# Softmax denominators from sums of four key tiles, and a planner with other durations

## The chip, the cores and the metric

The kernel runs on one core of a Trainium2 chip. Its time is the device time of one execution in microseconds (us). A core has five instruction queues that run beside each other: TensorE (PE; its weight loads are shown apart as PEld), VectorE (DVE), ScalarE (ACT), GpSimd (POOL) and SyncE (SP), which here issues the DMAs.

## The reference

One pre-norm transformer layer, S = 2048 tokens, D = 1024, 32 heads of 32, F = 3584, everything bf16 at its edges:

```
h  = x + softmax(q k^T / sqrt(32)) v @ wo      with q, k, v = layernorm(x) @ wqkv
h2 = h + (gelu_tanh(layernorm(h) @ w1 + b1) @ w2 + b2)
```

There is no mask; the layer norms have no scale and no offset.

## The kernel before

**Attention.** A job is one group `g` of four heads (4 x 32 = 128 rows) and one block `qb` of 256 queries; there are 8 x 8 = 64 jobs. A job has eight rounds `r`, each of two key tiles of 128 keys. A round first makes scores in `Att.qk` (line 769): eight matmuls, four at a time on 32-row strips of the array, into two of three score units of two PSUM banks (banks 0 to 5). Then two exponentials on ScalarE (line 779), one for each unit, 128 x 1024 each, write the probabilities to one of nine `PT` buffers. `Job.pv` (line 805) multiplies them with V, four matmuls at a time on 32-column strips, and accumulates into the left half of a bank (6 or 7); `Job.den` (line 834) multiplies them, or sums of them, with a matrix of ones, and accumulates the softmax denominators into the right half of the same bank. `Job.finish` (lines 850 to 865) transposes and inverts the denominators and scales the output on VectorE.

**The denominators.** For rounds 0 to 6 VectorE first adds the two key tiles of the round (the pair sum, line 820, 128 x 1024 bf16), into one of three `PS` buffers used in turn, and `den` then needs four matmuls for the round. Round 7 goes to `den` directly, with eight. The two jobs of the lead (`g` = 0, `qb` < 2) take all eight rounds directly. A sum that round r appends is handed to `den` in the call of `pv` for round r + 1, behind its value matmuls.

**The rest of the layer** is background work (kind "bg") that TensorE does between the rounds: the projections of Q, K and V, the output projection `wo(u)` of a block u of 256 tokens, `ln2(u)`, `ffn1(u)` and `ffn2(u)`. Their results leave PSUM through banks 6 and 7 only, mostly by VectorE (for `ffn1` line 943). The GELU of four 128-wide chunks is four VectorE instructions and one ScalarE tanh (lines 962 to 967, the tanh on 965), in two `uu` buffers. The last block's `wo(7)`, `ln2(7)`, `ffn1(7)`, `ffn2(7)` come after the last job and use all banks (line 540). In the lead (`lead_norm` and the loop over `hc`) the layer norms of x, the transposes, the first projections and the two lead jobs run interleaved.

**The planner.** Nothing of this order is written out. The kernel first builds a graph of tasks; each has an engine, a duration (`occ`), a latency until its result can be used (`lat`) and a priority. `Graph.schedule` then simulates the engines by these figures: when an engine comes free it takes the ready task of lowest priority number (pair sums have -2, PSUM evictions 0, GELU steps 1); TensorE's task is chosen by `pick_pe`: scores first, then a value round when three rounds wait, else background work. A change between strip shapes on TensorE costs `switch`. The order so found is emitted: five fixed queues, with semaphore waits between them. On the chip each engine works strictly down its queue, so a task whose input is late holds all that is queued behind it. The planner's figures come from the helper functions

```python
MM = 0.2195
def c_dve_ps(n): return (120 + n) / 960.0 + 0.02
def c_dve(n, x=1): return (62 + n / x) / 960.0 + 0.085
def c_act(n, ap_bias=False): return 0.073 + (0.093 if ap_bias else 0.0) + n / 1200.0
```

and from constants at the calls.

Of the kernel before, what the change touches and what calls it, by code (L numbers as in the profile page):

```python
# [60 lines left out]
class Graph:  # L61
# [46 lines left out]

    def schedule(self, pick_pe, pool, switch=0.1, dma_rate=280.0, dma_lat=2.1, dma_issue=0.06):
        for i, t in enumerate(self.tasks):  # L110
# [10 lines left out]
        n = 0  # L121
# [207 lines left out]
def build_kernel(nc, A_x, A_wqkv, A_wo, B_w1, B_b1, B_w2, B_b2, out):  # L329
# [156 lines left out]

    MM = 0.2195
    def c_dve_ps(n):
        return (120 + n) / 960.0 + 0.02

    def c_dve(n, x=1):
        return (62 + n / x) / 960.0 + 0.085

    def c_act(n, ap_bias=False):
        return 0.073 + (0.093 if ap_bias else 0.0) + n / 1200.0

    def pe(fns, occ, reads=(), writes=(), kind="bg", mode="full", prio=0, after=()):
        return gr.add(E.PE, fns, occ, 0.16, reads, writes, prio, kind, mode, after)

# [15 lines left out]
    def bb(bank):  # L515
        return bank.buf if isinstance(bank, Slot) else B_ps[bank]
# [10 lines left out]
    def mm(bank, lhsT, rhs, start, stop, reads, narrow, cols=(0, 512), after=()):  # L527

        c0, c1 = cols
        occ = MM * (c1 - c0) / 512.0 + 0.003  # L530
        if narrow:
            fns = []
            for j in range(4):
                fns.append(lambda p, j=j: p.matmul(psum[32 * j:32 * j + 32, bi(bank), c0:c1], lhsT[:, 32 * j:32 * j + 32], rhs,  # L534
                                                   start=start, stop=stop, tile_position=(0, 32 * j), skip_group_check=True))
            t = pe(fns, occ, reads=reads, writes=[bb(bank)], mode="col", after=after)
            t.whole = lambda p: p.matmul(psum[:, bi(bank), c0:c1], lhsT, rhs, start=start, stop=stop,  # L537
                                         skip_group_check=True)
        else:
            t = pe(lambda p: p.matmul(psum[:, bi(bank), c0:c1], lhsT, rhs, start=start, stop=stop),  # L540
                   occ, reads=reads, writes=[bb(bank)], mode="full", after=after)
        take(t, bank)

    def act(fn, n, reads=(), writes=(), prio=0, ap_bias=False, kind="", after=()):
        return gr.add(E.Activation, fn, c_act(n, ap_bias), 0.14, reads, writes, prio, kind, after=after)

    def dve(fn, occ, reads=(), writes=(), prio=0):
        return gr.add(E.DVE, fn, occ, 0.08, reads, writes, prio)

# [24 lines left out]
    def layer_norm(tiles, prio, norm="dve", stats=None):  # L574
# [6 lines left out]
        for k, (x_ap, B_x, o_ap, B_o) in enumerate(tiles):  # L581
            for c in range(2):
                dve(lambda v, c=c, k=k, x_ap=x_ap: v.bn_stats(st_l[:, i + k, 6 * c:6 * c + 6], x_ap[:, 512 * c:512 * c + 512]),
                    0.68, reads=B_x if isinstance(B_x, list) else [B_x], writes=[B_stl[i + k]], prio=(prio or 1) if stats is None else stats)
            dve(lambda v, k=k: v.bn_aggr(mv_l[:, i + k, :], st_l[:, i + k, :]), 0.2,  # L585
                reads=[B_stl[i + k]], writes=[B_mv[i + k]], prio=prio)
# [9 lines left out]
        for k, (x_ap, B_x, o_ap, B_o) in enumerate(tiles):  # L596
            eng, cost = (dve, 0.58) if norm == "dve" else (pool, 3.8)
            eng(lambda e, k=k, x_ap=x_ap, o_ap=o_ap: e.tensor_scalar(
                o_ap, x_ap, mvr[:, i + k, :], rden[:, i + k, :], ALU.subtract, ALU.mult), cost,
                reads=(B_x if isinstance(B_x, list) else [B_x]) + [B_mvr[i + k], B_rden[i + k]], writes=[B_o], prio=prio)  # L600

    def transposes(src_ap, B_src, bank, dst_ap, B_dst, evac, prio):
        for dc in range(DC):
            t = pe(lambda p, dc=dc: p.transpose(psb[:, bi(bank), dc * P:(dc + 1) * P], src_ap[:, dc * P:(dc + 1) * P], ident[:]),  # L604
                   0.064, reads=[B_src, B_ident], writes=[bb(bank)], prio=prio)
            take(t, bank)

        def src():
            return psb[:, bi(bank), :].rearrange("p (dc t) -> p dc t", dc=DC)
        if evac == "act":  # L610
            t = act(lambda a: a.activation(dst_ap, src(), ACT.Copy), 1024, reads=[bb(bank)], writes=[B_dst], prio=-1)  # L611
        else:
            t = dve(lambda v: v.tensor_copy(dst_ap, src()), 0.70, reads=[bb(bank)], writes=[B_dst])
        drop(t, bank)
# [132 lines left out]
    class Att:  # L747
# [8 lines left out]
        def qk(self, job, r):  # L756
# [16 lines left out]
            for u in us:  # L773
                banks += [B_ps[2 * u], B_ps[2 * u + 1]]
            pe(fns, 0.224, reads=[B_KT[8 * g + r], B_QT[qs]], writes=banks, kind="qk", mode="row")
            s = self.rounds % NR
# [9 lines left out]

    closing = set()

    class Job:
# [8 lines left out]
        def pv(self, r, s):  # L798
# [10 lines left out]
            rd = [B_PT[2 * s], B_PT[2 * s + 1], B_V[NT * g + 2 * r], B_V[NT * g + 2 * r + 1]]  # L809
            t = pe(fns, 0.224, reads=rd, writes=[self.B_O, self.B_D] if first else [self.B_O], kind="pv", mode="col")  # L810
            take(t, bank)
            while self.sums:
                self.den(*self.sums.pop(0), False)
            if r == 7 or (self.g == 0 and self.qb < 2):
                self.sums.append((s, True))
            else:
                n = cnt["ps"] % NS
                cnt["ps"] += 1
                pairs = PT[:, s, :, :, :].rearrange("p u j c -> p (u j) c")
                dve(lambda v: v.tensor_tensor(PS[:, n, :, :], pairs[:, :, 0:256], pairs[:, :, 256:512], ALU.add), c_dve(1024, 2),  # L820
                    reads=[B_PT[2 * s], B_PT[2 * s + 1]], writes=[B_PS[n]], prio=-2)
                self.sums.append((n, False))
            if last:
# [4 lines left out]
        def den(self, n, direct, last):  # L828
            bank = self.bank
            fns = []  # L830
            for i in range(2 if direct else 1):
                for h in range(4):
# [3 lines left out]
                        start=False, stop=last, tile_position=(0, 32 * h), skip_group_check=True))  # L836
            t = pe(fns, 0.224 if direct else 0.112, reads=[B_PT[2 * n], B_PT[2 * n + 1]] if direct else [B_PS[n]],
                   writes=[self.B_D], kind="den", mode="col")
# [3 lines left out]
        def finish(self):  # L842
# [6 lines left out]
            D = OD[:, o, 1, :].rearrange("p (b j) -> p b j", j=32)  # L849
            t = dve(lambda v: v.transpose(OD[:, o, 1, :], psum[:, bi(bank), 256:512]), 0.445,  # L850
                    reads=[self.B_O, self.B_D], writes=B_D, prio=-1)
# [7 lines left out]
            drop(t, bank)  # L859
            dve(lambda v: v.reciprocal(rr[:, o, :], D[:, :, 0]), 0.185, reads=B_D, writes=[B_rr[o]], prio=0)  # L860
            dve(lambda v: v.transpose(D, rr[:, o, :].unsqueeze(2).to_broadcast([P, 8, 32])), c_dve(256),
# [144 lines left out]
    for k in range(80):  # L1006
        pe(lambda p: p.matmul(psum[:, 6, 0:256], ident[:, :], b2t[:, 0:256], start=True, stop=True), 0.12,  # L1007
           reads=[B_ident, B_b2t], writes=[B_ps[6]], kind="warm")
# [243 lines left out]
```

## Time and profile before

| what | value |
|---|---|
| median of 3 runs | 1100.69 us (1100.36, 1100.69, 1102.47) |
| profiled execution, span of its instructions | 1099.2 us; its own time is given by this span alone, 1.5 us under the median of the runs |
| instructions | 42056 |
| TensorE busy | 1056.5 us, 96% |
| ScalarE busy | 1019.8 us, 93% |
| VectorE busy | 757.2 us, 69% |
| GpSimd busy | 47.8 us, 4% |
| first exponential starts, last exponential starts | 16.4 us, 1030.0 us |
| ScalarE idle before the exponentials, in all | 18.2 us |

A busy TensorE in this table is not TensorE at its peak: the matmuls overlap and their ends are modelled. "Idle before" is time in which the engine stood still ahead of an instruction, with what ended it. The exponentials of one queue overlap by their start-up, so their durations (some 1.2 us) add up to more than the time that they take: one follows the other every 0.92 us.

### The profile page before, as it was taken

The numbers are of one execution on the slowest core, as the hardware profiler recorded it, in microseconds if no ns is written. First come the engines' busy times: TensorE is split into PE (matmuls) and PEld (weight loads), VectorE is DVE, ScalarE is ACT, GpSimd is POOL, SyncE is SP. The second block draws the span as 40 slices with busy tenths as digits, with TensorE's granted clock in tenths as the row PEclk, the third lists the DMA queues.
The fourth block names the chain that finished last, engine by engine and source line by source line (L and its number), as shares of the span: only waits on it lengthen the run. The fifth ranks groups of instructions, "written<-read, shape, count | busy, mean of one in ns | idle before, by whom it ended". The sixth has DMA issues, their size and how long they took to land.

```text
span 1099.2 us, 42056 instructions
## 1 busy us (share of the span) xinstructions
PE 1056.5 (96%) x19177; PEld 613.8 (56%) x19226; DVE 757.2 (69%) x1444; ACT 1019.8 (93%) x1124; POOL 47.8 (4%) x110
## 2 busy tenths in 40 slices
PE   8899999998899999999999899999999999999998
PEld 6655555553345744664475456546744664565483
DVE  7746666665676886788588768876886787687501
ACT  3879999999999999999999999999999999999650
POOL 3200000000000001001000100010010000000100
PEclk9999999999899999999999999999999999999999
DMA  6820000048345654854576466448654747797370
GB/s 184 227 103 2 29 2 3 2 159 268 115 122 154 189 151 150 260 162 149 185 228 188 150 203 180 143 150 255 181 178 149 216 142 239 243 266 242 98 262 20
DMA packets 265506, 174.43 MB, mean 159 GB/s; under 512 B 26864, under 2 KB 260336, under 8 KB 264560
## 3 DMA queue, kind: packets, MB, share of 16 engines
q1 hardware_dynamic: 265328, 171.74, 51.2%
q8 instruction: 151, 2.47, 0.9%
q14 instruction: 27, 0.22, 0.1%
HBM read 161.23 MB, written 10.49 MB: 156 GB/s over the span
## 4 chain that ended last, share of the span: by engine, by line
ACT 79%; PE 19%; DVE 1%; issue 0%; DMA 0%; POOL 0%; POOLq 0%; DVEq 0%
ACT PT L779 75%; PE ps L540 6%; ACT uu L965 4%; PE ps L537 4%; PE ps L534 3%; PE ps L769 2%; PE ps L805 1%; PE ps L1007 1%; PE ps L834 1%; DMA a_w1r<-in_A_wo_dram 0%; ACT xnT L611 0%; PE ps L604 0%; DVE PS L820 0%; DVE OD L850 0%; DVE OD L857 0%
## 5 line engine op out<-in xcount | busy, mean ns | idle before, releaser
L779 ACT ACTIVATE PT<-ps 128x1024 bf16<-128x1024 f32 x1024 | 953.6, 1189 | 18.2 <-PE ps L769 18.0
L820 DVE TENSOR_TENSOR PS<-PT 128x1024 bf16<-128x1024 bf16 x434 | 287.5, 686 | 124.5 <-ACT PT L779 63.8
L769 PE MATMUL ps<-QT,KT 32*128 32x256 bf16 x4096 | 204.6, 273 | 13.5 <-ACT PT L779 10.2
L805 PE MATMUL ps<-PT,V 128*32 128x256 bf16 x4096 | 179.9, 273 | 1.5 <-ACT PT L779 1.1
L769 PEld LDWEIGHTS ps<-QT,KT 32*128 32x128 bf16 x4096 | 61.0, 92 | 174.1 <-ACT PT L779 165.3
L834 PE MATMUL ps<-PS,ones 128*32 128x256 bf16 x1736 | 121.7, 274 | 2.0 <-DVE PS L820 2.0
L805 PEld LDWEIGHTS ps<-PT,V 128*32 128x32 bf16 x4096 | 103.8, 97 | 30.0 <-issue 8.7
L537 PE MATMUL ps<-a_w2r,gT 128*128 128x512 bf16 x445 | 109.6, 380 | 4.9 <-issue 2.4
L537 PE MATMUL ps<-hnT,a_w1r 128*128 128x256 bf16 x903 | 111.2, 273 | 1.1 <-DVE rr L860 0.5
L534 PE MATMUL ps<-hnT,a_w1r 128*32 128x256 bf16 x2660 | 96.9, 274 | 2.4 <-DVE gT L943 1.2
L537 PEld LDWEIGHTS ps<-hnT,a_w1r 128*128 128x128 bf16 x903 | 82.7, 98 | 25.1 <-issue 14.8
L943 DVE TENSOR_TENSOR gT<-ps,b1f 128x512 bf16<-128x512 f32 x98 | 67.3, 687 | 27.7 <-PE ps L534 18.4
L534 PE MATMUL ps<-a_w2r,gT 128*32 128x512 bf16 x1140 | 81.6, 381 | 2.5 <-DVE OD L857 2.5
L534 PEld LDWEIGHTS ps<-hnT,a_w1r 128*32 128x32 bf16 x2660 | 66.2, 96 | 18.5 <-issue 14.0
L537 PEld LDWEIGHTS ps<-a_w2r,gT 128*128 128x128 bf16 x471 | 40.4, 98 | 55.3 <-issue 15.7
L989 DVE SCALAR_TENSOR_TENSOR hch<-ps,hch 128x512 bf16<-128x512 f32 x32 | 22.0, 689 | 64.0 <-PE ps L540 47.1
L834 PEld LDWEIGHTS ps<-PS,ones 128*32 128x32 bf16 x1736 | 45.9, 96 | 22.8 <-issue 8.7
L965 ACT ACTIVATE uu<-uu 128x1024 bf16<-128x1024 bf16 x49 | 58.0, 1206 | 0.0
L537 PE MATMUL ps<-xnT,Wall 128*128 128x512 bf16 (+1 forms) x213 | 47.7, 360 | 2.3 <-issue 1.1
L588 POOL CAST mvb<-mv 128x2 bf16<-128x2 f32 (+1 forms) x25 | 6.1, 242 | 990.0 <-DVE mv L585 987.2
L706 DVE CAST V<-ps 128x512 bf16<-128x512 f32 x32 | 22.1, 690 | 30.8 <-PE ps L537 15.8
L537 PE MATMUL ps<-Wall,xnT 128*128 128x256 bf16 x327 | 41.0, 273 | 0.0
(85 smaller groups left out, 1009.8 us busy)
## 6 DMA issues: line engine op xcount, KB each, us to landing
a_w2r<-in_B_w_dram SPq DMA_DIRECT2D x105, 512.0 KB, 5.6
a_w1r<-in_B_w_dram SPq DMA_DIRECT2D x98, 512.0 KB, 4.4
a_w1r<-in_A_wo_dram SPq DMA_DIRECT2D x32, 512.0 KB, 4.0
b_w1r<-in_B_w_dram SPq DMA_DIRECT2D x14, 512.0 KB, 5.8
a_w1r<-in_A_wqkv_dram SPq DMA_DIRECT2D x11, 512.0 KB, 4.3
xrb<-in_A_x_dram SPq DMA_DIRECT2D x16, 256.0 KB, 4.2
Wall<-in_A_wqkv_dram SPq DMA_DIRECT2D x16, 256.0 KB, 4.8
hch<-in_A_x_dram SPq DMA_DIRECT2D x16, 256.0 KB, 4.0
```

Of the source, the lines that this page charges most:

```text
L534: fns.append(lambda p, j=j: p.matmul(psum[32 * j:32 * j + 32, bi(bank), c0:c1], lhsT[:, 32 * j:32 * j + 32], rhs, start=start, stop=stop, ...
L537: t.whole = lambda p: p.matmul(psum[:, bi(bank), c0:c1], lhsT, rhs, start=start, stop=stop, skip_group_check=True)
L540: t = pe(lambda p: p.matmul(psum[:, bi(bank), c0:c1], lhsT, rhs, start=start, stop=stop), occ, reads=reads, writes=[bb(bank)], mode="full" ...
L706: t = dve(lambda v: v.tensor_copy(dst, psum[:, bi(bank), :].rearrange("p (t g c) -> p g t c", t=2, g=2)), c_dve_ps(512), reads=[bb(bank)], ...
L769: return p.matmul(psum[:, 2 * us[h // 2] + h % 2, 256 * i:256 * i + 256], KT[32 * h:32 * h + 32, g, k0:k0 + P], QT[32 * h:32 * h + 32, qs, :],
L779: act(lambda a, u=u, k=k: a.activation(PT[:, s, k, :, :], psum[:, 2 * u:2 * u + 2, :], ACT.Exp, bias=0.0, scale=SCALE), 1024, reads=[B_ps[ ...
L805: fns.append(lambda p, i=i, h=h: p.matmul(psum[32 * h:32 * h + 32, bi(bank), 0:256], V[:, g, 2 * r + i, 32 * h:32 * h + 32], PT[:, s, h // ...
L820: dve(lambda v: v.tensor_tensor(PS[:, n, :, :], pairs[:, :, 0:256], pairs[:, :, 256:512], ALU.add), c_dve(1024, 2), reads=[B_PT[2 * s], B_ ...
L834: fns.append(lambda p, h=h, rhs=rhs, i=i: p.matmul(psum[32 * h:32 * h + 32, bi(bank), 256:512], ones32[:, :], rhs, start=False, stop=last, ...
L943: t = dve(lambda v: v.tensor_tensor(g[:, fc:fc + 2, :], psum[:, bi(bank), :].rearrange("p (f c) -> p f c", f=2), b1f[:, fc:fc + 2].unsquee ...
L965: act(lambda a: a.activation(w, w, ACT.Tanh, bias=0.0, scale=KT2), 1024, reads=[B_uu[i]], writes=[B_uu[i]], prio=-1)
L989: drop(dve(lambda v, hs=hs, bank=bank, half=half: v.scalar_tensor_tensor(hch[:, hs, c], psum[:, bi(bank), :], half, hch[:, hs, c], ALU.mul ...
```

## The change

Rounds 0 to 5 of a job outside the lead now go in pairs of rounds. The pair sum of round 0, 2 or 4 is kept in its `PS` buffer. After the pair sum of round 1, 3 or 5 VectorE adds the kept buffer to it, in place, and one `den` of four matmuls serves both rounds. Round 6 keeps its pair sum and its own `den`, round 7 stays direct. And the planner's durations and latencies are replaced; this alters no instruction by itself, only the order in which the five queues are filled. The diff, with the unchanged lines cut:

```diff
-    def schedule(self, pick_pe, pool, switch=0.1, dma_rate=280.0, dma_lat=2.1, dma_issue=0.06):
+    def schedule(self, pick_pe, pool, switch=0.104, dma_rate=280.0, dma_lat=2.1, dma_issue=0.06):
...
-    MM = 0.2195
+    MM = 0.21333
     def c_dve_ps(n):
-        return (120 + n) / 960.0 + 0.02
+        return (120 + n) / 960.0 - 0.058
     def c_dve(n, x=1):
-        return (62 + n / x) / 960.0 + 0.085
+        return (62 + n / x) / 960.0
     def c_act(n, ap_bias=False):
-        return 0.073 + (0.093 if ap_bias else 0.0) + n / 1200.0
+        return (0.064 if n == 1024 else 0.073) + (0.093 if ap_bias else 0.0) + n / 1200.0
     def pe(fns, occ, reads=(), writes=(), kind="bg", mode="full", prio=0, after=()):
-        return gr.add(E.PE, fns, occ, 0.16, reads, writes, prio, kind, mode, after)
+        return gr.add(E.PE, fns, occ, 0.225 if isinstance(fns, list) and len(fns) > 1 else 0.2, reads, writes, prio, kind, mode, after)
...
-        occ = MM * (c1 - c0) / 512.0 + 0.003
+        occ = MM * (c1 - c0) / 512.0 + 0.0026
...
     def act(...):   # latency
-        return gr.add(E.Activation, fn, c_act(n, ap_bias), 0.14, ...)
+        return gr.add(E.Activation, fn, c_act(n, ap_bias), 0.16, ...)
     def dve(...):   # latency
-        return gr.add(E.DVE, fn, occ, 0.08, reads, writes, prio)
+        return gr.add(E.DVE, fn, occ, 0.135, reads, writes, prio)
...
-  bn_stats 0.68,  normalize on VectorE 0.58,  transpose 0.064,   its eviction 0.70
+  bn_stats 0.595, normalize on VectorE 0.334, transpose 0.0565,  its eviction 0.615
-  qk 0.224, pv 0.224, den 0.224 or 0.112, den transpose 0.445, reciprocal 0.185, warm-up matmul 0.12
+  qk 0.222, pv 0.22,  den 0.22 or 0.11,   den transpose 0.36,  reciprocal 0.1,   warm-up matmul 0.109
...
+    FOURS = (0, 2, 4)
...
                 dve(lambda v: v.tensor_tensor(PS[:, n, :, :], pairs[:, :, 0:256], pairs[:, :, 256:512], ALU.add), c_dve(1024, 2),
                     reads=[B_PT[2 * s], B_PT[2 * s + 1]], writes=[B_PS[n]], prio=-2)
-                self.sums.append((n, False))
+                if r in FOURS:
+                    self.half = n
+                elif r - 1 in FOURS:
+                    o = self.half
+                    dve(lambda v: v.tensor_tensor(PS[:, n, :, :], PS[:, n, :, :], PS[:, o, :, :], ALU.add), c_dve(1024, 2),
+                        reads=[B_PS[n], B_PS[o]], writes=[B_PS[n]], prio=-2)
+                    self.sums.append((n, False))
+                else:
+                    self.sums.append((n, False))
```

The lines of constants between "bn_stats" and "warm-up matmul" stand for one edit each at the call in question.

More of the change, by code (lines that the diff above doesn't have):

```diff
@@ L544, in act @@
     def act(fn, n, reads=(), writes=(), prio=0, ap_bias=False, kind="", after=()):
-        return gr.add(E.Activation, fn, c_act(n, ap_bias), 0.14, reads, writes, prio, kind, after=after)
+        return gr.add(E.Activation, fn, c_act(n, ap_bias), 0.16, reads, writes, prio, kind, after=after)
     def dve(fn, occ, reads=(), writes=(), prio=0):
-        return gr.add(E.DVE, fn, occ, 0.08, reads, writes, prio)
+        return gr.add(E.DVE, fn, occ, 0.135, reads, writes, prio)
     def pool(fn, occ, reads=(), writes=(), prio=0):
@@ L583, in layer_norm @@
                 dve(lambda v, c=c, k=k, x_ap=x_ap: v.bn_stats(st_l[:, i + k, 6 * c:6 * c + 6], x_ap[:, 512 * c:512 * c + 512]),
-                    0.68, reads=B_x if isinstance(B_x, list) else [B_x], writes=[B_stl[i + k]], prio=(prio or 1) if stats is None else stats)
+                    0.595, reads=B_x if isinstance(B_x, list) else [B_x], writes=[B_stl[i + k]], prio=(prio or 1) if stats is None else stats)
             dve(lambda v, k=k: v.bn_aggr(mv_l[:, i + k, :], st_l[:, i + k, :]), 0.2,
@@ L596, in layer_norm @@
         for k, (x_ap, B_x, o_ap, B_o) in enumerate(tiles):
-            eng, cost = (dve, 0.58) if norm == "dve" else (pool, 3.8)
+            eng, cost = (dve, 0.334) if norm == "dve" else (pool, 3.8)
             eng(lambda e, k=k, x_ap=x_ap, o_ap=o_ap: e.tensor_scalar(
@@ L604, in transposes @@
             t = pe(lambda p, dc=dc: p.transpose(psb[:, bi(bank), dc * P:(dc + 1) * P], src_ap[:, dc * P:(dc + 1) * P], ident[:]),
-                   0.064, reads=[B_src, B_ident], writes=[bb(bank)], prio=prio)
+                   0.0565, reads=[B_src, B_ident], writes=[bb(bank)], prio=prio)
             take(t, bank)
@@ L612, in transposes @@
         else:
-            t = dve(lambda v: v.tensor_copy(dst_ap, src()), 0.70, reads=[bb(bank)], writes=[B_dst])
+            t = dve(lambda v: v.tensor_copy(dst_ap, src()), 0.615, reads=[bb(bank)], writes=[B_dst])
         drop(t, bank)
@@ L774, in qk @@
                 banks += [B_ps[2 * u], B_ps[2 * u + 1]]
-            pe(fns, 0.224, reads=[B_KT[8 * g + r], B_QT[qs]], writes=banks, kind="qk", mode="row")
+            pe(fns, 0.222, reads=[B_KT[8 * g + r], B_QT[qs]], writes=banks, kind="qk", mode="row")
             s = self.rounds % NR
@@ L809, in pv @@
             rd = [B_PT[2 * s], B_PT[2 * s + 1], B_V[NT * g + 2 * r], B_V[NT * g + 2 * r + 1]]
-            t = pe(fns, 0.224, reads=rd, writes=[self.B_O, self.B_D] if first else [self.B_O], kind="pv", mode="col")
+            t = pe(fns, 0.22, reads=rd, writes=[self.B_O, self.B_D] if first else [self.B_O], kind="pv", mode="col")
             take(t, bank)
@@ L836, in den @@
                         start=False, stop=last, tile_position=(0, 32 * h), skip_group_check=True))
-            t = pe(fns, 0.224 if direct else 0.112, reads=[B_PT[2 * n], B_PT[2 * n + 1]] if direct else [B_PS[n]],
+            t = pe(fns, 0.22 if direct else 0.11, reads=[B_PT[2 * n], B_PT[2 * n + 1]] if direct else [B_PS[n]],
                    writes=[self.B_D], kind="den", mode="col")
@@ L849, in finish @@
             D = OD[:, o, 1, :].rearrange("p (b j) -> p b j", j=32)
-            t = dve(lambda v: v.transpose(OD[:, o, 1, :], psum[:, bi(bank), 256:512]), 0.445,
+            t = dve(lambda v: v.transpose(OD[:, o, 1, :], psum[:, bi(bank), 256:512]), 0.36,
                     reads=[self.B_O, self.B_D], writes=B_D, prio=-1)
@@ L859, in finish @@
             drop(t, bank)
-            dve(lambda v: v.reciprocal(rr[:, o, :], D[:, :, 0]), 0.185, reads=B_D, writes=[B_rr[o]], prio=0)
+            dve(lambda v: v.reciprocal(rr[:, o, :], D[:, :, 0]), 0.1, reads=B_D, writes=[B_rr[o]], prio=0)
             dve(lambda v: v.transpose(D, rr[:, o, :].unsqueeze(2).to_broadcast([P, 8, 32])), c_dve(256),
@@ L1006, in build_kernel @@
     for k in range(80):
-        pe(lambda p: p.matmul(psum[:, 6, 0:256], ident[:, :], b2t[:, 0:256], start=True, stop=True), 0.12,
+        pe(lambda p: p.matmul(psum[:, 6, 0:256], ident[:, :], b2t[:, 0:256], start=True, stop=True), 0.109,
            reads=[B_ident, B_b2t], writes=[B_ps[6]], kind="warm")
```

## The prediction

> **What bounds the kernel now.** I read the busy times by stage first, with the stages cut at the first exponential (16.4), at the last gap of the lead (71.2) and at the end of the exponentials (1031), then the same stages for lines 779 and 965 alone, then the chain.
>
> ```profile
> core 0: us, PE busy (x) PEld busy (x) DVE busy (x) ACT busy (x) POOL busy (x), PEclk, DMA share, GB/s
> 16.40:71.20 54.80, 50.07 (x1119) 35.60 (x1119) 35.16 (x81) 39.76 (x42) 10.54 (x23) 1.00 0.65 191
> 71.20:1031.00 959.80, 927.75 (x17512) 526.87 (x17554) 699.14 (x1315) 956.52 (x1041) 26.72 (x56) 1.00 0.52 158
> 1031.00:1099.20 68.20, 64.77 (x434) 40.29 (x439) 11.49 (x23) 19.43 (x37) 3.40 (x8) 1.00 0.37 125
> ```
>
> ```profile
> 71.21 208.25 ACT PT L779 x227
> ...
> 1034.08 5.34 PE ps L540 x24
> 1039.42 0.86 PE ps L537 x4
> 1040.29 0.22 PE ps L540
> ...
> 1046.12 25.75 PE ps L540 x230
> ```
>
> The chain (start, length, what) runs on ScalarE without a break for 227 exponentials: 208.25 / 227 = 0.917 us each. The middle stage holds 1041 ScalarE instructions (992 exponentials, 49 tanhs of the same size): 1041 x 0.917 = 955.0 of 959.8 us. So in the middle ScalarE leaves only 4.8 us, whatever TensorE does. Ahead of it lies a lead of 71.2 us in which both TensorE (50.1 of 54.8 us) and ScalarE's inputs pace, behind it a tail of 68.2 us that the chain gives to TensorE.
>
> ```profile
> DVE PS L820 <- ACT PT L779: 63.8, 99, 2.5
> DVE PS L820 <- PE ps L834: 57.0, 66, 5.1
> ...
> ACT PT L779 <- PE ps L769: 18.0, 16, 3.8
> ```
>
> The table of waits (who waited <- for whom: us in total, times, the longest) shows how little ScalarE waits for scores, and what line 820 waits for; part 2 comes back to it.
>
> **Part 1, matmuls removed.** 62 jobs make 62 x 7 = 434 pair sums; three per job no longer go to `den`: 186 groups of four matmuls and four weight loads, 1488 instructions of 42056. The chain gives such a group 0.11 us ("PE ps L834 x4" beside value matmuls; they stand between column-strip work, so no switch goes with them). 186 x 0.11 = 20.5 us of TensorE. Nearly all of it lies beside ScalarE, which is full. What ScalarE can get is what it lost to TensorE's order in the middle, at most 4.8 us. I went through its gaps: about 1.9 near 280 is the clock dip below, 0.8 near 697 a wait for the `wo` weights' DMA, 1.2 near 854 a stop of TensorE with no visible cause ("issue"); those stay. The small ones near 384, 792 and 966 (0.4 each) are TensorE late with the scores, and those go: **-1.2 us**, ends 0 and -4.8.
>
> **Part 2, adds put in.** 186 adds of 128 x 1024 bf16 from SBUF to SBUF. Not in the trace in place, but line 964 is the same form and also in place:
>
> ```profile
> L964 DVE TENSOR_TENSOR uu<-uu,gT 128x1024 bf16<-128x1024 bf16 x49 | 33.3, 685 | 0.3
> ```
>
> 0.685 us alone, and 0.62 in a row (seven line-820 sums from 1018.41 take 4.41: (4.41 - 0.69) / 6). 186 x 0.62 = 115 us; VectorE goes from 757 to 872 us, in the middle from 699 to 814 of 960, 85%. Does it fit where it is dense?
>
> ```profile
> 375.00:400.00 25.00, 24.84 (x515) 15.31 (x507) 21.49 (x41) 24.91 (x28) 0.00 (x0) 1.00 0.55 158
> 400.00:425.00 25.00, 24.15 (x357) 11.32 (x353) 21.98 (x46) 25.00 (x28) 4.74 (x8) 1.00 0.72 220
> 425.00:450.00 25.00, 24.55 (x446) 12.47 (x446) 13.08 (x26) 25.00 (x28) 0.00 (x0) 1.00 0.53 172
> ```
>
> 25 us hold some 13.5 rounds, so 5 adds, 3.1 us: 24.6 and 25.1 of 25 by these two dense rows (busy counts 0.08 us of overlap at each isolated instruction, so about 23.6), and 16 in the third. Full in the `ffn1` stretches, with room a stretch later. The adds have the highest priority, GELU steps a low one, so GELU is what slips; `ffn2` needs it last. I take 0 for this in the middle; if the cover is gone it is the rival below.
>
> The adds also change the ring of three `PS` buffers, to which 57 us of VectorE waiting go. Before, the sum of round 3 needs `den` of round 0. Now round 3 takes the kept buffer of round 0, free since the add, and only round 4 waits, for the `den` of rounds 0 and 1, issued behind the value matmuls of round 2. Rounds 4, 5 and 6 still fall into the value burst: three sums and an add, against four sums. No new stall of `den`; 0.
>
> **Part 3, the planner.** Against the trace: a pair sum in a row 0.62 (planned 0.683, now 0.598), line 943 0.61 in a row (0.678, now 0.600), normalizing 0.46 (0.58, now 0.334), an exponential 0.917 (0.926, now 0.917), a 512-column matmul 0.216 (0.2225, now 0.2159). So the old plan thought VectorE 10 to 25% slower than it is and TensorE 3%; the new one is within a few per cent, but thinks VectorE 1 to 4% faster than it is. In the lead the old error shows: VectorE stands in its queue at eight V evictions (line 706) for 11.1 us, waiting for TensorE, with layer-norm steps queued behind; ScalarE loses 15.0 us to late scores there. TensorE is busy 50.1 of 54.8 us, so 4.7 us is the most that a better order gives, and a worse one may cost as much. Nearer to the gain, as the blocked queue follows from the wrong figures: **-1.3 us**.
>
> **Part 4, the tail.** Its 68.2 us are TensorE's, with the block's `ffn1` and `ffn2` fixed. Five matmuls of `ffn2(6)` are left over from before (0.86 + 0.22 us at 1039.4), and their eviction at 1040.33 holds up the last `bn_stats` by 0.9 us. The last two jobs save 6 x 0.11 = 0.66 us ahead of it, three of the five. **-0.4 us**, ends -0.9 and +1 (five more left over).
>
> Sum: -1.2 - 1.3 - 0.4 = -2.9 us on a span of 1099.2, so 1096.3; with the 1.5 us that lie between this span and the median, **1097.8 us**. 0.2%, about what a measurement of this kernel can tell from no change, is 2.2 us: faster is below 1098.5, slower above 1102.9.
>
> **Rivals.**
>
> *No change (1100.2).* All 20.5 us of TensorE vanish beside ScalarE: the gaps near 384, 792 and 966 turn up elsewhere with a new order, the lead comes out as it was, only 0.5 us of the tail goes. For it: 955.0 of 959.8. Against: the queue blocked in the lead.
>
> *VectorE sets the tanhs (1104.5).* A tanh stands in ScalarE's queue where the plan thinks its input ready; if VectorE is late, all exponentials behind it wait, which the old, slow figures kept from happening (idle before line 965: 0.0). Lag: some 40 instructions in a dense 25 us, each 0.007 to 0.022 us over the new figure, is 0.3 to 0.9 us. With the plan's margin spread evenly over 0 to 0.917 us, a lag of L costs L x L / (2 x 0.917) for each of 49 tanhs: 2.4 us at 0.3, 6.7 at 0.5. Taking 0.5: -2.9 + 6.7 = +3.8. It decides above L = 0.44 us, where the loss passes 2.9 + 2.2. For it: VectorE full in these stretches. Against: it is idle in each stretch after, so the lag does not add up from block to block, and a late ScalarE lets VectorE catch up.
>
> *The clock (1107).* Where background work runs out, TensorE's clock falls:
>
> ```profile
> 272.00:276.00 4.00, 2.54 (x56) 0.90 (x52) 2.37 (x4) 4.00 (x6) 0.00 (x0) 1.00 0.98 336
> 276.00:280.00 4.00, 2.00 (x40) 0.60 (x32) 2.22 (x6) 4.00 (x5) 0.00 (x0) 0.70 0.33 100
> 280.00:284.00 4.00, 4.00 (x20) 1.15 (x17) 1.38 (x2) 3.24 (x5) 0.00 (x0) 0.50 0.01 4
> 284.00:288.00 4.00, 4.00 (x43) 1.48 (x45) 2.03 (x3) 3.22 (x4) 0.00 (x0) 0.95 0.00 0
> ```
>
> Half busy for 8 us, then a granted clock of 0.50, and when work returns ScalarE idles 0.76 + 0.78 = 1.5 us. Less work on TensorE means more such stretches: one in each of the six `ffn` blocks is 6 x 1.5 = 9.2 us, -2.9 + 9.2 = +6.3. Against: the shares there are 23.0 of 25 us at the least, and a block of some 102 us loses 20.5 x 102 / 960 = 2.2 us of work. The Trainium skill says, in "TensorE: Matmul & The Clock Gate", Part 1, that TensorE falls to half clock after an idle window of about 3.4 us; the trace agrees on the half (0.50) but not on the condition, since its longest stop from 272 to 280 is 1.2 us. By the page the change would cost nothing here, as no stretch of 3.4 us is idle; by the row, half-busy stretches are enough.
>
> *The lead gets longer (1103.8).* Normalizing is now planned at 0.334 against 0.46, over 16 tiles 2.0 us too early; transposes queued too early on TensorE hold the scores. At its worst the 1.3 us are not gained and the 4.7 are lost: -2.9 + 1.3 + 4.7 = +3.1.
>
> That rounds 0 to 5 do not pair up can be left out: `pv` comes in the order of r, so round 0 always sets the kept buffer.
>
> **Chances.** Forecast 0.42, no change 0.28, tanhs 0.21, clock 0.04, lead 0.05. So faster 0.42, same 0.28, slower 0.30. Low end: the whole 4.8, 2 of the lead and 0.4 of the tail, -7.2: 1093.5. High end: the tanhs at L a little above 0.5: 1105.5; about 0.06 lie below and 0.12 above. The forecast's own range is 1093.5 to 1098.5.
>
> **What would show it.** Right: 992 line-834 matmuls from `PS` in place of 1736, 620 adds into `PS` in place of 434; middle stage 957 to 959 us; idle before line 965 under 1 us; line 706's wait in the lead under 11.1 us; clock below 1 only around 280. Wrong: idle before line 965 of several us, a middle stage above 961 us, a lead over 72 us, a tail over 69 us, or the clock at 0.5 in an `ffn` block.

## The result and the profile after

The change made the kernel slower: 1108.55 us (median of 6 runs, 1107.42 to 1109.60) against 1100.53 us for the kernel before (6 runs, 1099.28 to 1103.94). The ratio on record is 1.0063, with a 95% interval of 1.0051 to 1.0075 (the plain quotient of the two medians, 1.0073, lies near its upper end). The profiled execution took 1109.4 us, its span is 1107.6 us, so the middle, the lead and the tail can be set against those of before by their spans. Behind the added lines the numbers shift: line 834 of before (`den`) is now 843, line 965 (tanh) is 974, the pair sum is on line 821 and the new add on 827.

The stages of after, cut at the same events as before (first exponential, last gap of the lead, end of the exponentials):

```profile
16.40:68.20 51.80, 48.13 (x1061) 34.97 (x1062) 34.04 (x77) 39.76 (x42) 10.28 (x22) 1.00 0.71 202
68.20:1038.70 970.50, 918.21 (x16648) 509.03 (x16692) 812.13 (x1505) 959.74 (x1041) 29.80 (x56) 0.98 0.51 156
1038.70:1107.60 68.90, 65.09 (x431) 40.16 (x434) 10.80 (x22) 19.55 (x37) 3.40 (x8) 0.98 0.37 122
```

The lead ends 3.0 us earlier (71.2 to 68.2), the tail is 0.7 us longer (68.2 to 68.9), and the middle is 10.8 us longer (959.7 to 970.5). ScalarE's 1041 instructions still need 955.0 us of it, so ScalarE's slack there rose from 4.8 to 15.5 us, while TensorE's busy time in the middle fell by 9.5 us. The granted clock of the middle and the tail is 0.98 where it was 1.00.

The costly groups of the changed lines (busy and mean ns of one; idle before them, and what ended it):

```profile
L821 DVE TENSOR_TENSOR PS<-PT 128x1024 bf16<-128x1024 bf16 x434 | 294.7, 685 | 83.5 <-ACT PT L779 63.7
L827 DVE TENSOR_TENSOR PS<-PS 128x1024 bf16<-128x1024 bf16 x186 | 127.7, 687 | 3.8
...
L843 PE MATMUL ps<-PS,ones 128*32 128x256 bf16 x992 | 70.1, 277 | 4.8 <-issue 2.3
...
L974 ACT ACTIVATE uu<-uu 128x1024 bf16<-128x1024 bf16 x49 | 54.3, 1108 | 0.0
```

The change is what it says: 434 + 186 = 620 instructions write `PS`, and 992 `den` matmuls read it in place of 1736. The tanhs of line 974 never wait (0.0), so the rival in which VectorE is late with GELU did not happen. In the table of waits, `PS` sums wait far less for `den` (14.9 us, 57.0 before):

```profile
DVE PS L821 <- ACT PT L779: 63.7, 82, 3.3
...
ACT PT L779 <- PE ps L769: 22.9, 25, 4.0
...
DVE PS L821 <- PE ps L843: 14.9, 34, 1.8
```

What is new is the clock. In stretches of 4 us (duration; busy time and count of PE, PEld, DVE, ACT, POOL; then the granted clock, the DMA share and GB/s), these rows stand out; before had a clock under 0.95 only from 276 to 284:

```profile
244.00:248.00 4.00, 2.49 (x37) 0.83 (x38) 2.21 (x7) 4.00 (x6) 0.00 (x0) 0.76 1.08 315
...
272.00:276.00 4.00, 3.44 (x52) 1.10 (x48) 1.49 (x3) 4.00 (x6) 0.00 (x0) 0.50 0.06 16
276.00:280.00 4.00, 2.75 (x24) 0.85 (x21) 3.39 (x8) 4.00 (x6) 0.00 (x0) 0.50 0.00 0
280.00:284.00 4.00, 4.00 (x18) 1.11 (x16) 1.60 (x3) 2.31 (x3) 0.00 (x0) 0.55 0.01 4
...
944.00:948.00 4.00, 2.04 (x28) 0.47 (x25) 3.09 (x8) 2.52 (x3) 1.81 (x4) 0.50 0.48 134
...
1032.00:1036.00 4.00, 3.01 (x44) 0.66 (x36) 2.37 (x4) 4.00 (x6) 0.00 (x0) 0.50 0.00 0
1036.00:1040.00 4.00, 3.45 (x28) 1.05 (x30) 1.38 (x2) 2.91 (x4) 0.00 (x0) 0.50 0.44 129
```

Reading the row of 280 to 284: TensorE is busy all of it, but with 18 matmuls at about half speed, and ScalarE has 2.31 us of work in 4.00. From 266.2 to 278.5 us TensorE has no background work at all. The trace's record of the clock holds only the values 1 and 0.5, so a mean clock of 0.980 over 1107.6 us is 2 x 0.020 x 1107.6 = 44 us at half clock; before, with 0.997, it was 7 us. This measure, "half-clock time", is used below.

I went through ScalarE's gaps of the middle, 12.8 of the 15.5 us in 13 places. About 4.5 us stand where the clock is low (249, 279, 283, 895, 950; the one at 895 also stands behind a wait of 1.8 us for a block of `w2`); before it was 1.9. Some 2.6 us more (825, 942) begin behind late steps of VectorE, on lines 598, 613 and 998, but the matmuls that follow run at half clock, from 822.9 to 826.3 and from 942.4 on, so the two causes can't be parted there. About 1.2 us follow from VectorE's order alone, as the timeline shows (start, length, what, and in brackets the idle time ahead of it and what ended it):

```profile
820.73 0.65 DVE L827 TENSOR_TENSOR PS<-PS 128x1024 bf16<-128x1024 bf16 x1
821.29 0.42 DVE L866 COPY OD<-ps 128x256 f32<-128x256 f32 x1
...
821.77 0.62 PE L604 MATMUL ps<-ident,a_xb 128*128 128x128 bf16 x8 [2.21 <-DVE OD L866]
...
822.77 1.02 ACT L779 ACTIVATE PT<-ps 128x1024 bf16<-128x1024 f32 x1 [0.91 <-PE ps L769]
```

The add (priority -2) goes ahead of the eviction of a job's bank on line 866 (priority -1); TensorE's transposes need that bank and stand 2.21 us, and the scores queued behind them come late. And about 4.3 us follow stops of TensorE in which it waited for nothing that the profile shows, as here:

```profile
542.72 0.28 PE L843 MATMUL ps<-PS,ones 128*32 128x256 bf16 x2 [1.36 <-issue]
543.39 1.94 ACT L779 ACTIVATE PT<-ps 128x1024 bf16<-128x1024 f32 x2 [1.18 <-PE ps L769]
```

There were seven such stops of over 0.25 us in this profile, 4.9 us in all, against three with 2.5 us before. So one profile offers three causes: the clock, VectorE's order, and the stops. The experiments try to tell them apart.

### The profile page after: what moved, and what is told of

Its sections match the earlier page's. It is cut to its first block, busy times and chain, and to the rows that moved or that the text cites. A ratio compares the mean times of both kernels' runs of the same rounds, so it can differ in the third digit from the quotient of the medians.

```text
span 1107.6 us, 40413 instructions
## 1 busy us (share of the span) xinstructions
PE 1045.3 (94%) x18252; PEld 595.4 (54%) x18302; DVE 868.5 (78%) x1630; ACT 1023.1 (92%) x1124; POOL 50.9 (5%) x110
## 4 chain that ended last, share of the span: by engine, by line
ACT 55%; PE 36%; DVE 6%; POOL 1%; issue 1%; DMA 0%; POOLq 0%; DVEq 0%; SPq 0%
ACT PT L779 52%; PE ps L537 12%; PE ps L534 7%; PE ps L540 6%; PE ps L769 5%; PE ps L806 3%; ACT uu L974 2%; DVE PS L821 2%; PE ps L843 1%; PE ps L1016 1%; DVE st L583 1%; PE ps L604 1%; POOL denb L592 0%; DMA a_w2r<-in_B_w_dram 0%; DVE PS L827 0%
## 5 line engine op out<-in xcount | busy, mean ns | idle before, releaser
L821 DVE TENSOR_TENSOR PS<-PT 128x1024 bf16<-128x1024 bf16 x434 | 294.7, 685 | 83.5 <-ACT PT L779 63.7
L806 PE MATMUL ps<-PT,V 128*32 128x256 bf16 x4096 | 173.2, 277 | 2.9 <-ACT PT L779 2.6
L827 DVE TENSOR_TENSOR PS<-PS 128x1024 bf16<-128x1024 bf16 x186 | 127.7, 687 | 3.8
L537 PE MATMUL ps<-a_w2r,gT 128*128 128x512 bf16 x476 | 119.1, 385 | 8.4 <-issue 2.1
L537 PE MATMUL ps<-hnT,a_w1r 128*128 128x256 bf16 x943 | 115.8, 273 | 1.9 <-DVE OD L866 0.8
L534 PE MATMUL ps<-hnT,a_w1r 128*32 128x256 bf16 x2500 | 91.7, 274 | 6.2 <-DVE OD L866 1.9
L952 DVE TENSOR_TENSOR gT<-ps,b1f 128x512 bf16<-128x512 f32 x98 | 67.1, 685 | 10.8 <-PE ps L534 8.3
L843 PE MATMUL ps<-PS,ones 128*32 128x256 bf16 x992 | 70.1, 277 | 4.8 <-issue 2.3
L534 PEld LDWEIGHTS ps<-hnT,a_w1r 128*32 128x32 bf16 x2500 | 60.6, 96 | 25.1 <-issue 18.4
L534 PE MATMUL ps<-a_w2r,gT 128*32 128x512 bf16 x1008 | 71.5, 382 | 0.9 <-DVE OD L866 0.9
L534 PE MATMUL ps<-xnT,Wall 128*32 128x512 bf16 (+1 forms) x648 | 39.3, 354 | 0.2
```

What stands on the lines that cost most here:

```text
L806: fns.append(lambda p, i=i, h=h: p.matmul(psum[32 * h:32 * h + 32, bi(bank), 0:256], V[:, g, 2 * r + i, 32 * h:32 * h + 32], PT[:, s, h // ...
L827: dve(lambda v: v.tensor_tensor(PS[:, n, :, :], PS[:, n, :, :], PS[:, o, :, :], ALU.add), c_dve(1024, 2), reads=[B_PS[n], B_PS[o]], writes ...
L843: fns.append(lambda p, h=h, rhs=rhs, i=i: p.matmul(psum[32 * h:32 * h + 32, bi(bank), 256:512], ones32[:, :], rhs, start=False, stop=last, ...
L952: t = dve(lambda v: v.tensor_tensor(g[:, fc:fc + 2, :], psum[:, bi(bank), :].rearrange("p (f c) -> p f c", f=2), b1f[:, fc:fc + 2].unsquee ...
```

## The experiments

Each ratio is the time against the kernel before on the same chip, where its median was 1101.5 to 1102.7 us, with its 95% interval. Lead, middle and tail are from one profile each.

### Which half of the change

**The durations alone** (`plan_only`), an edit to after:

```diff
-    FOURS = (0, 2, 4)
+    FOURS = ()
```

> The new durations without the sums of four (every round keeps its own pair sum and den, as before). Three theories of the 8 us: (A) TensorE, with 20.5 us less to do, runs out of work, its clock falls to half, and scores come late; (B) VectorE, with 115 us more to do, falls behind the plan, and TensorE stands at banks and sums that the plan thought ready; (C) the order that the new durations give is itself worse. A and B: the load is as before, so the shorter lead (3 us) shows alone, 1096 to 1100 us. C: 1105 to 1110 us.

Measured: 1104.25 us, 1.0026 (1.0007 to 1.0044). Lead end 68.0, middle 967.2, tail 68.8; half-clock time 31 us. The lead's gain comes whole from the durations, and so does part of the middle's loss.

**The sums of four alone, with the old durations** (`fours_only`): before, plus the diff's part in `Job.pv`.

> The sums of four with the old durations. A: TensorE lacks the same 20.5 us of work, so the clock falls as often, and without the shorter lead it is 1107 to 1112 us. B: the old plan thinks VectorE 10 to 25% slower than it is, so VectorE keeps ahead of it in spite of the adds, 1099 to 1104 us. C: 1098 to 1101 us.

Measured: 1177.91 us, 1.0683 (1.0644 to 1.0723). The middle is 964.9, but the tail is 142.3 us. The table of waits shows why:

```profile
ACT uu L974 <- DVE uu L973: 49.6, 7, 30.5
```

The tanhs wait 49.6 us in 7 places, 30.5 in one, and all seven lie behind the last exponential, from 1069.5 to 1094.9 us: they are GELU work that the plan left for the tail, and no exponential stands behind them. The planner counts each add at 0.683 us where it takes 0.62; by its figures VectorE overflows, GELU is planned later and later, and some 74 us of background work are left for the tail. This is not what the adds cost on the chip, as the next run shows.

**The sums with VectorE's figures new, TensorE's and ScalarE's old** (`fours_dve`), and **VectorE's figures alone** (`dve_new`), **the other figures alone** (`pe_act_new`), both without the sums:

> Sums of four with VectorE's new figures, and TensorE's and ScalarE's old ones. With the old VectorE figures the sums of four took 1178 us; if that was the plan's belief that VectorE is full, it goes: under 1112 us. Margin theory: 1100 to 1105 us, better than the changed kernel; without it, 1106 to 1112 us.

> The kernel before with VectorE's durations and latency alone set to the new ones; TensorE's and ScalarE's stay (3% and 1% slower than the trace). If the margin in TensorE's and ScalarE's figures is what kept the middle close to 955 us, the middle stays near 960 and the lead gets shorter by up to 3 us: 1097 to 1101 us. If VectorE's figures spoil the middle, 1102 to 1106 us.

> The other half: new figures for TensorE, ScalarE and the switch, old ones for VectorE. Margin on TensorE and ScalarE is the protection: a middle of 964 to 968 us and the old lead, 1103 to 1108 us. VectorE's figures spoil the middle: 1099 to 1102 us.

Measured: `fours_dve` 1107.62, 1.0057 (1.0041 to 1.0074), middle 968.3: the overflow is gone, and with the old TensorE and ScalarE figures it is as slow as after. So too tight a margin in those figures is not what makes after slow. `dve_new` 1.0006 (0.9989 to 1.0023), lead end 70.1; `pe_act_new` 1.0035 (1.0018 to 1.0051), lead end 74.4, 3 us later than before. Neither half of the figures gives the lead of 68.0; both together do.

### Does the adds' own time cost anything, and has TensorE room

**Adds of a 32nd** (`short_adds`): after's queues, each add on 8 of 256 columns, so the denominators lack most of the kept sum.

```diff
-  v.tensor_tensor(PS[:, n, :, :], PS[:, n, :, :], PS[:, o, :, :], ALU.add)
+  v.tensor_tensor(PS[:, n, :, 0:8], PS[:, n, :, 0:8], PS[:, o, :, 0:8], ALU.add)
```

> The changed kernel with the order of all queues kept, but each of the 186 adds works on 8 of 256 columns (most of the add is left out), about 0.1 us in place of 0.6. VectorE is relieved of about 90 us, TensorE has as little as in the changed kernel. A: nothing comes back, 1106 to 1110 us. B: the middle comes back, 1096 to 1101 us. C: nothing comes back, 1106 to 1110 us.

Measured: 1107.75, 1.0057 (1.0040 to 1.0074), middle 970.4. With nearly all of the adds' time taken away in the same order (VectorE's busy time falls from 868.5 to 783.3 us), the middle stays. VectorE's load is not the cause; what its order does is kept in this run.

**TensorE's work given back** (`pe_back`): after's queues, with four zero-weight matmuls into the same sum ahead of each `den` that serves two rounds; 186 x 0.11 = 20.5 us of TensorE.

> The changed kernel with the order of all queues kept, but each den of a sum of four is preceded by four matmuls with weights of zero, so TensorE has its 186 groups (20.5 us) back while VectorE keeps the adds. A: the clock holds, 1098 to 1103 us. B and C: nothing is gained and TensorE comes later still, 1107 to 1113 us.

Measured: 1128.84, 1.0242 (1.0205 to 1.0280), middle 990.8. The 20 us cost 20 us. So work put on TensorE behind the planner's back is not hidden by ScalarE. Two things qualify this. The profile has ten unexplained stops with 10.3 us, against 4.9 in after, so a part of the 20 us may be theirs. And its clock is 0.982, hardly above the 0.980 of after: against what theory A expected, work given back in these places does not hold the clock. Work taken off *with* the planner's knowledge is another matter: the planner then moves background work forward, and TensorE runs out of it later. The traces show the shift: of all columns that the matmuls of the projections and of `ffn` stream, 78.0% have started by 900 us in before (half-clock time 7 us), 79.5% in after (44 us), 80.0% in `plan_only` (31 us), and, of the next two runs, 81.5% in `relief` (53 us) and 77.7% in `adds` (4 us). The kernels that run ahead are those whose clock is low.

**Only the relief** (`relief`: after without the line-827 adds, so that a `den` covers one round of two) and **only the adds** (`adds`: all seven `den`s as before, and 186 extra VectorE instructions of the add's form that leave the sum as it is):

```diff
  relief
-                    o = self.half
-                    dve(lambda v: v.tensor_tensor(... PS[:, o, :, :], ALU.add), c_dve(1024, 2), ..., prio=-2)
  adds
-                    self.half = n
+                    self.sums.append((n, False))
...
-  v.tensor_tensor(PS[:, n, :, :], PS[:, n, :, :], PS[:, o, :, :], ALU.add)
+  v.tensor_tensor(PS[:, n, :, :], PS[:, n, :, :], PS[:, n, :, :], ALU.max)
```

> New durations and the dens of the sums of four, but without the 186 adds, also in the plan (the keys of rounds 0, 2 and 4 are left out of the denominators). TensorE has as little to do as in the changed kernel, VectorE as little as before. A (too little work on TensorE, the clock): as bad as the changed kernel, 1106 to 1110 us, with several stretches at half clock. B' (the adds crowd VectorE's queue already in the plan, so that evictions, layer norms and GELU come later): like the new durations alone or better, 1099 to 1105 us.

> New durations, all seven dens of a job as before, and 186 extra VectorE instructions of the add's size and priority (the maximum of a sum with itself, which changes nothing), planned like the adds. TensorE has as much to do as before, VectorE as much as in the changed kernel. A: like the new durations alone, 1101 to 1106 us. B': as bad as the changed kernel or worse, since TensorE has no slack either, 1107 to 1115 us.

Measured: `relief` 1106.93, 1.0045 (1.0028 to 1.0062), middle 968.3; `adds` 1107.36, 1.0053 (1.0033 to 1.0072), middle 968.8. Taking 20 us of work from TensorE and adding nothing is slower than `plan_only` by its median, not faster, though the intervals overlap. So do those of `adds` and `plan_only`: with full traffic these runs do not say which half of the sums of four costs the time. The mean clocks tell the two apart:

```profile
core 0: 1105.7 us, clock 0.976
```

```profile
core 0: 1105.5 us, clock 0.998
```

The first line is `relief` (53 us at half clock), the second `adds` (4 us). `adds` loses its time otherwise: eight unexplained stops with 3.7 us, and a gap of 3.3 us at 125.8 that belongs to its own order (`adds_light`, below, has it too).

**Evictions ahead of the adds** (`evict_first`): the evictions of `finish` at priority -3.

```diff
-                    reads=[self.B_O, self.B_D], writes=B_D, prio=-1)
+                    reads=[self.B_O, self.B_D], writes=B_D, prio=-3)
```

> The changed kernel, but the two evictions of Job.finish get priority -3, ahead of the pair sums and adds (-2), so that the bank of a finished job comes free sooner. In the changed kernel TensorE stood 2.2 us at 821.8 for such an eviction, and ScalarE lost some 2 us there. If such waits carry the loss, 1102 to 1106 us; if they are a small part of it, 1106 to 1109 us.

Measured: 1107.44, 1.0046 (1.0031 to 1.0061). Its interval overlaps that of after; bank waits like the one at 821.8 may be worth a part of a microsecond or two, but this run does not resolve it.

### The unexplained stops

Many stand where the DMA engines are full, as in this row of after around the stop shown above (DMA share 1.10, 84 matmuls):

```profile
540.00:544.00 4.00, 2.64 (x84) 1.99 (x84) 1.29 (x2) 2.82 (x4) 0.00 (x0) 1.00 1.10 370
```

**Light traffic** (`light_dma`): after, where each weight block of `w1`, `w2`, `wo` and the later Q weights that goes into a buffer once filled brings only a quarter of its data.

```diff
+            d = 2 if R is R1 and ("w1", s) in filled else DC
+            filled.add(("w1", s))
-  dma(R.w1[:, s, :, :], src_ap.rearrange(...), ...)
+  dma(R.w1[:, s, 0:d, :], src_ap.rearrange(...)[:, 0:d, :], ...)
...  (w2 in the same way, 1 of 4)
```

> The changed kernel with the order of all queues kept, but every weight block of wo, the late Q projections, ffn1 and ffn2 (until the last block's own ring) after the first filling of its buffer brings only a quarter of its data (the rest of the block is left out and stays as it was). (D) TensorE's stops of 0.3 to 1.4 us that no instruction explains (the page's 'issue'; seven in the changed kernel, 4.9 us) come where the DMA engines are fully busy and TensorE has bursts of narrow matmuls: then they go with the load, and 3 to 5 us come back, 1103 to 1106 us; the wait for a w2 block near 888 goes too. If the stops have nothing to do with the load, they stay, and at most that one wait is gained, 1106 to 1109 us.

Measured: 1105.1, 1.0025 (1.0014 to 1.0036); two stops with 0.65 us are left of seven with 4.9. That looked like the cause. The same edit to the durations alone (`plan_light`), and, as a control, to the kernel before (`before_light`):

> The new durations alone (no sums of four), order kept, with a quarter of each later weight block as in light_dma (three quarters of these blocks are left out). If the stops of TensorE beside full DMA engines are what the new order alone loses (ratio 1.0026), they go, and the shorter lead (3 us) shows: 1096 to 1100 us. If the order loses in other ways, 1100 to 1104 us.

> The kernel before with a quarter of each later weight block (three quarters left out), order kept. Its middle has one unexplained stop (near 854, 1.2 us of ScalarE) and one wait for a block (near 697, 0.8 us), and one stop in the lead that lies ahead of this traffic: at most 2 us are to be had, 1098 to 1101 us. If the traffic costs more than the stops, e.g. in every matmul, under 1097 us.

Measured: `plan_light` 1099.67, 0.9979 (0.9965 to 0.9993); `before_light` 1097.32, 0.9958 (0.9942 to 0.9974). The kernel before gains as much: full against light traffic costs 0.42% in before, 0.47% in the durations alone, 0.38% in after. So the full traffic costs these three about the same 0.4%, some 4.5 us, and that after's profile shows more stops does not explain its loss. This reading fell. Nor is all of the 0.4% stops: in before, the profiles show three with 2.5 us with full traffic and one with 1.4 us with light traffic, while the small gaps near 384, 697, 792 and 966 us go as well.

**Fewer transfers in flight** (`plan_lanes`: `plan_only` with `N_LANES` 6 in place of 24):

> The new durations alone, all data loaded, with 6 transfers in flight in place of up to 24 (the planner and the semaphores know of 6 lanes). If the stops come from many large transfers in flight, they go and it is faster than before, 1096 to 1100 us; if six are enough to fill the DMA engines as now, as the new durations alone, 1102 to 1106 us; if weights come late, over 1106 us.

Measured: 1105.96, 1.0035 (1.0020 to 1.0050), ten stops with 6.8 us. A miss: fewer transfers at a time do not take the stops away.

The traces say more about the stops. In all twenty profiles together, past their first 20 us, there are 80 of over 0.25 us, with 61 us. 66 of them, with 53 us, end 1.2 to 1.6 us after a transfer on one of the DMA queues that the profile marks "instruction" has landed, as the one at 542.72 us does, 1.42 us after; if the two had nothing to do with each other, about five would. So most stops look like waits of TensorE for its instructions. No run changed these transfers alone, so this is not tested.

Light traffic still has a use: it takes most of the stops out of the comparison. **The two halves under light traffic** (`relief_light`, `adds_light`):

> The run relief (new durations, dens of four, no adds, so that the keys of rounds 0, 2 and 4 are missing from the denominators) with a quarter of each later weight block. A (too little work on TensorE, its clock): 1102 to 1105 us, as light_dma. B' (VectorE): as the new durations alone with light traffic, 1098 to 1101 us.

> The run adds (new durations, all dens, 186 extra VectorE instructions) with a quarter of each later weight block. A: 1098 to 1101 us. B': 1102 to 1106 us.

Measured, all with light traffic, each against the kernel before with full traffic:

| kernel | ratio | step | half-clock time, us |
|---|---|---|---|
| `before_light` | 0.9958 (0.9942 to 0.9974) | | 7 |
| `plan_light`: new durations | 0.9979 (0.9965 to 0.9993) | +0.21% | 26 |
| `relief_light`: and less TensorE work | 1.0028 (1.0017 to 1.0039) | +0.49% | 53 |
| `adds_light`: new durations and the adds | 0.9999 (0.9985 to 1.0012) | +0.20% | 7 |
| `light_dma`: new durations and both | 1.0025 (1.0014 to 1.0036) | +0.46% | 44 |

Steps count from the ratio above for the durations, and from `plan_light` for the last three. The loss of the change is 0.67% here and 0.63% with full traffic, the same within the intervals. With light traffic, most of what the sums of four add to it comes with the lighter TensorE alone: for `relief_light` and `light_dma` the intervals lie clear above `plan_light`'s, for `adds_light` they overlap. With full traffic the steps over `plan_only` are +0.19% for `relief` and +0.27% for `adds`, neither clear of nothing; light traffic gave `relief` 0.17% and `adds` 0.54%. One rival is left untested: each kernel of this table has an order of its own, and a new order alone moved the time by 0.06% (`dve_new`) to 0.35% (`pe_act_new`), so a step of 0.2% may be no more than that. A run that takes TensorE's work out of the order of before, and leaves that order as it is, would decide it; it was not made. The same stretch in two of these kernels, `relief_light` first:

```profile
904.00:908.00 4.00, 3.28 (x52) 0.98 (x44) 1.23 (x3) 4.00 (x5) 0.00 (x0) 0.50 0.24 82
912.00:916.00 4.00, 4.00 (x27) 1.14 (x26) 1.71 (x3) 2.23 (x3) 0.00 (x0) 0.72 0.02 4
```

```profile
904.00:908.00 4.00, 3.72 (x53) 1.51 (x56) 3.48 (x9) 4.00 (x6) 0.00 (x0) 1.00 0.19 66
912.00:916.00 4.00, 4.00 (x79) 2.11 (x79) 1.54 (x3) 4.00 (x6) 0.00 (x0) 1.00 0.26 62
```

With 27 slow matmuls TensorE fills the 4 us from 912 in `relief_light`, and ScalarE gets 2.23 us of work; `before_light` does 79 in the time, and ScalarE is full.

### Is it the clock

**TensorE kept busy where the clock fell** (`light_warm`): `light_dma` with 16 zero-weight matmuls ahead of the values of rounds 1 to 6 in three jobs, those at about 250, 270 and 1030 us.

```diff
+    WARM = ((1, 6), (0, 7), (7, 7))
...
+            if (self.qb, g) in WARM and not first and not last:
+                for k in range(16):
+                    fns.insert(0, lambda p, k=k: p.matmul(... zero32[:, :], PT[...], start=False, stop=False, ...))
```

> light_dma (the changed kernel's order, a quarter of each later weight block) with 16 matmuls by weights of zero, 0.43 us at full clock, ahead of the value matmuls of rounds 1 to 6 in three jobs whose stretches ran at half clock: (1, 6), (0, 7) and (7, 7). A (the clock is the cause): the clock is 1.0 near 250 to 285 and 1025 to 1040, and 2 to 4 us come back from light_dma's 1105.1, that is 1101 to 1103 us. If the low clock only goes with something else (banks, layer norms), the added work delays scores further, 1105 to 1109 us.

Measured: 1103.33, 1.0010 (1.0000 to 1.0019), against 1.0025 (1.0014 to 1.0036) for `light_dma`. The intervals still overlap by 0.05%, but the profile shows the gain in its place. `light_dma`, and then `light_warm`:

```profile
272.00:276.00 4.00, 3.43 (x52) 1.08 (x48) 1.60 (x3) 4.00 (x5) 0.00 (x0) 0.50 0.06 16
...
280.00:284.00 4.00, 4.00 (x18) 1.15 (x17) 1.71 (x3) 2.33 (x3) 0.00 (x0) 0.52 0.02 4
1032.00:1036.00 4.00, 3.62 (x28) 1.06 (x30) 1.29 (x2) 2.75 (x3) 0.00 (x0) 0.50 0.45 131
```

```profile
272.00:276.00 4.00, 3.09 (x84) 1.76 (x87) 2.41 (x4) 4.00 (x5) 0.00 (x0) 1.00 0.13 38
...
280.00:284.00 4.00, 3.83 (x37) 1.46 (x37) 2.83 (x6) 4.00 (x6) 0.00 (x0) 1.00 0.00 0
1032.00:1036.00 4.00, 3.70 (x56) 1.79 (x58) 1.09 (x2) 2.21 (x3) 0.00 (x0) 1.00 0.46 131
```

More work for TensorE, and the clock stays at 1.00; 37 matmuls go through from 280 to 284 in place of 18, and ScalarE is full there (4.00 against 2.33). ScalarE's 2.5 us of gaps at 279 to 283 are gone and the tail falls from 69.3 to 67.5. The added work costs a gap of 1.3 us of its own at 256.6, and the dips at 816, 888 and 936 to 948, which it did not treat, remain. So a low clock is a cause here, of some 4 us in the places treated by this profile, of which 1.6 us net (0.15% of 1100) were won back, a step that the intervals do not quite part from nothing.

**The same in the kernel before** (`before_warm`, job (0, 7) alone, all data), as a version that might beat both:

> The kernel before, all data, with the same 16 matmuls in job (0, 7) alone, ahead of its one stretch at half clock (276 to 288), where ScalarE lost 1.8 us. A: the stretch stays at full clock and 1 to 2 us are gained, ratio 0.998 to 0.999. Otherwise 1.000 to 1.003.

Measured: 1105.34, 1.0033 (1.0020 to 1.0046). A miss: the dip moved to 280 to 284, and its profile has six stops with 5.6 us. No version that ran with all data beats the kernel before.

## Why the prediction was wrong

It said 1097.8 us, faster; it is 1108.55 us, slower and above the range. Against its own steps:

- **Middle, -1.2 us; measured +10.8.** This is the step that failed. Part 1 priced 20.5 us less TensorE work as free at worst ("Nearly all of it lies beside ScalarE, which is full"). The price was not zero: with light traffic `relief_light` puts it at 0.49%, some 5 us, in an order of its own, while `relief` with full traffic does not resolve it (+0.19%). TensorE then runs short of work in more stretches, the clock falls (44 us at half clock in after, 7 before), and the scores, and at the end of the last job the tail, come late when work returns. `light_warm` keeps the order and lifts the clock, and ScalarE's gaps in the treated places go: the clock is a cause of them, and not only a sign. It won back 1.6 us; how much of the +10.8 us the clock carries in all is not shown.
- **The clock rival had the mechanism right and the chance wrong, and its time is near in part by luck.** 1107 us was priced with 1.5 us for each of six dips, and given 0.04, because 25-us averages showed TensorE busy for 23.0 us at the least. In after there are six dips, of 3.4 to 13.7 us, but they sit at the ends of the projections, at a change of blocks and in the last job, not one in each `ffn` block, and ScalarE's gaps beside them grew by 2.6 to 5.2 us in the profile, not by 9.2; the stops after which ScalarE idles (4.3 us against 1.2) make up much of the rest. A busy share over 25 us hides them: from 225 to 250 us after shows TensorE busy for 22.75 of 25 us, though it is busy for only 1.97 of the 3.40 us from 242.7 to 246.1, and the clock falls there.
- **The rule weighed there.** What counts is the stretch ahead of a fall. In after the clock falls at 270.0 us, and in the 3.4 us ahead of it, at full clock, TensorE is busy for 1.89 us with no stop of over 0.52 us:

```profile
266.60:270.00 3.40, 1.89 (x36) 0.58 (x36) 2.20 (x5) 3.40 (x5) 0.00 (x0) 1.00 0.87 297
270.00:273.40 3.40, 2.28 (x32) 0.66 (x36) 1.81 (x4) 3.40 (x5) 0.00 (x0) 0.50 0.49 151
```

In `light_warm`, with the added matmuls, the 6.8 us from 266.0 have TensorE busy for 2.99 and 2.77 of 3.40 us, and the clock stays at 1.00. The Trainium skill says, in "TensorE: Matmul & The Clock Gate", Part 1, that the clock falls after an idle window of about 3.4 us; these rows do not agree, since TensorE is partly busy in them. By that rule the change would have cost nothing here.

- **Adds, 0 in the middle.** Right on their time (`short_adds`: same middle) and on the `PS` ring (waits 57.0 to 14.9 us). Their place in VectorE's queue costs the wait at 821.8 (1.2 us of ScalarE); whether it costs more is open, since the 0.20% of `adds_light` does not exclude nothing. VectorE rose by 868.5 - 757.2 = 111.3 us, against 115 expected.
- **Planner and lead, -1.3 us; measured -3.0.** Right sign, too small. The named place carries little of it: line 706 waits 10.2 us in the lead, 11.1 before. What the prediction left out is that the durations order the middle too: `plan_light` stands 0.21% above `before_light`, with intervals that just overlap, although its lead is 2.3 us shorter than `before_light`'s (68.0 against 70.3), for its middle is 3.7 us longer (960.5 against 956.8).
- **Tail, -0.4 us; measured +0.7.** The last job ran at half clock from 1032 to 1040; with the clock kept up there the tail was 67.5.
- **Tanhs late, 0.21.** It did not happen in after (0.0 us at line 974), nor with the old durations: the 49.6 us of `fours_only` lie in its tail, where no exponential is held up.

What stays open: whether the unexplained stops are waits for instructions, as the landing times suggest, and why they become fewer with a quarter of the weight traffic but not with fewer transfers in flight. And of the 5 us or so that the sums of four cost under light traffic, `light_warm` won back 1.6 net; how the rest divides between the dips left, VectorE's order and the luck of a new order was not separated.

## What to carry to other kernels

Where two engines are both nearly full, taking work from one need not be free: look at the granted clock in stretches of a few microseconds, where work already runs thin, before calling the saving hidden. A planner's durations are part of the schedule: with VectorE's old durations, 10 to 25% too long, the sums of four made this kernel 6.8% slower (`fours_only`), with corrected ones 0.57% (`fours_dve`), and the whole set of corrected durations without the sums was itself 0.26% slower than the old set (`plan_only`). And an experiment that lightens a load says nothing until the kernel before has had the same lightening.

## What the runs showed of the hardware that was not expected

- In all twenty profiles the low clock comes in stretches of whole multiples of 3.41 us (one to six), all on one grid of that step in a profile, except where the kernel ends. Cut on this grid, without their first 20 and last 8 us, the profiles hold 74 windows at full clock that are followed by a fall, and in these TensorE is busy for 22 to 64% by the records. Each of the 15 windows under 45% was followed by a fall, none above 64% was, and between the two 59 were and 60 were not. So the window need not be idle, and the busy share alone does not decide it.
- At half clock a matmul lasts longer, so the busy share there says less: 86% from 272 to 276 in after, and the clock stays at 0.50.
- TensorE stops of 0.3 to 2.4 us, waiting for nothing that the profile's waits show; 66 of 80 end 1.2 to 1.6 us after an instruction transfer has landed. A quarter of the later weight traffic took them in after from 4.9 to 0.65 us.
- Sixteen matmuls with zero weights in a round, where TensorE ran short of work, kept the clock up (`light_warm`: 1.00 from 272 to 284); work added beside other work cost its full time and did not lift the clock (`pe_back`: 20 us for 20 us, clock 0.982). In the kernel before the same work cut the one dip from 6.8 to 3.4 us and gained nothing (`before_warm`: 1.0033).
